# Eight-row loads for Q and K of two batches, exponents in key order, and ones matmuls at the start of a fused attention and feed-forward kernel

## The chip, the cores and the metric

The kernel runs on one core of a Trainium2 chip. A core has five engines with a queue each: TensorE (PE; its weight loads are shown as PEld), VectorE (DVE), ScalarE (ACT), GpSimd (POOL) and SyncE (SP). SP and POOL issue the DMAs, which run on the core's 16 DMA engines. The metric is device time in microseconds: 335.08 us is the median of three runs of the kernel before, which lay between 334.21 and 335.22.

## The reference

Inputs are q, k and v of eight batches, eight heads, 576 positions and 64 channels, two weight matrices (512 x 2048 and 2048 x 512) and two scalars s and b. Attention sees a window of 32 positions to each side, and its output, 4608 rows of 512, goes through a feed-forward layer:

```python
scores = scale * np.matmul(q, k.transpose(0, 1, 3, 2))
mask = np.abs(pos[:, None] - pos[None, :]) <= window          # window = 32
attn = softmax(where(mask, scores, -1e9))                     # (written out in the reference)
x = (attn @ v).transpose(0, 2, 1, 3).reshape(B * S, H * D)
h = x @ w_in
g = s * np.maximum(h, 0.0) ** 2 + b
out = g @ w_out
```

## The kernel before

**Tiling.** Heads are handled in four pairs, so that a pair's 128 channels fill TensorE's rows. Keys lie in nine tiles of 64; a tile of keys meets a window of up to 128 queries. A unit (`unit`, L534) is two key tiles (the fifth has one): for each tile, four matmuls (one for each pair) write the scores into one of two banks of PSUM, SC (L543); ACT takes the exponent into EXE or EXO (L560); then matmuls with V and a column of ones (L582) give the output and the sums (AV), DVE divides (L592, L595), and the result goes, transposed, into XT, from which the feed-forward layer reads. The keys of a pair stand in KBD, block-diagonally: head 0 in the upper 64 rows and columns, head 1 in the lower ones. Batches 0 and 1 add the band mask on TensorE before the scores (a matmul of the identity with MASKB, L549) and transpose on TensorE (L604, L607); batches 2 to 7 multiply by a mask on DVE (L564) and transpose by DMA (L612).

**Loading Q and K.** Batches 0 and 1 use `pairs_chunk` (L451): three chunks of 256, 256 and 64 positions, for all heads at once, with two neighbouring positions per partition, so a packet is 512 bytes and a chunk fills 128, 128 or 32 partitions. Staging buffer STG (nine), a cast into NAT (six), eight transposes on TensorE (L473) into a bank, and copies into QT (L479) and KBD (L490, L491). The copies into KBD write with a step of two, so that keys stand in their order; QT keeps even and odd positions apart. Batches 2 to 7 use `chunk` (L496): the same chunks, a cast on DVE (L506), a transposing DMA (L514) and copies into KBD (L521), in which even and odd keys stay apart. The exponent reads a score tile as it lies (even queries, then odd ones) and writes with a step of two. V is loaded for each head into VST (L432) and cast into VBD (L445, L446).

**The feed-forward layer.** Blocks of 128, 128, 256 and then 512 tokens. `s1` (L687) multiplies XT by w_in (L698), ACT takes the Relu (L705), DVE squares it into GT (L707). `s2` (L711) multiplies GT by w_out (L717), DVE scales and adds the constant row (L730), SP stores (L734). The constant row comes from the column sums of w_out (L740, L744). For the first three blocks the second product is made in two halves of 256 columns, as the halves of w_out come in.

**What sets the order.** Every piece of work is a task with a stream (engine), an assumed cost, reads, writes and a key. `_order` (L113) simulates the engines with the assumed costs and takes again and again the task that can start first, and among equal starts the one with the lowest key; `_rings` (L87) estimates when the DMAs land. This gives each engine its instructions in a fixed order, with semaphore waits where needed. An engine that waits holds everything behind it in its queue. Loads of batch 2 and on wait for the AV matmuls of a unit of the batch before, chosen by the tables PACE (Q and K, issued by SP) and PACEV (V, issued by POOL) (L22, L23). The first loads have rising keys from -199 on: Q and K of batch 0, V of batch 0, w_in, s and b, one half of w_out, Q, K and V of batch 1, the other half of w_out. V of batch 1 waits, besides, for the landing of one w_out load. Fills of VBD, EXO and KBD, the identity and the masks are made in the first microseconds.

Of the kernel before, what the change touches and what calls it, by code (L numbers as in the profile page):

```python
# [10 lines left out]
S = 576  # L11
# [8 lines left out]
VW = 132  # L20
XTS = 4000.0
PACE = ((0, 0, 1, 2, 3, 3), (0, 0, 1, 2, 3, 3), (0, 1, 2, 3, 3, 3))  # L22
PACEV = ((0, 0, 1, 1), (0, 0, 1, 1), (0, 1, 2, 2))  # L23
# [4 lines left out]
class _Task:  # L28
    __slots__ = ("n", "stream", "fns", "cost", "lat", "key", "deps", "users", "left",
                 "ready", "start", "fin", "dma", "sem", "seq", "val", "used", "snap", "slack")  # L30

    def __init__(self, n, stream, fns, cost, lat, key, dma, slack):
        self.slack = slack
# [9 lines left out]
class _Graph:  # L43
# [7 lines left out]
    def __init__(self, queues):  # L51
        self.queues = queues
        self.tasks = []
        self.writer, self.readers = {}, {}

    def add(self, stream, fns, cost, reads=(), writes=(), key=0.0, accum=False, dma=None, waits=(),
            lat=None, slack=0.0):
        if not isinstance(fns, list):
            fns = [fns]
        t = _Task(len(self.tasks), stream, fns, cost, self.LAT[stream] if lat is None else lat, key,  # L60
                  dma, slack)
        t.deps.update(waits)
        for r in reads:
# [14 lines left out]
        self.tasks.append(t)  # L78
        return t
# [33 lines left out]
    def _order(self):  # L113
        free = {s: 600.0 for s in self.STREAMS}
        for t in self.tasks:
            t.left = len(t.deps)
# [6 lines left out]
        while len(order) < len(self.tasks):  # L123
# [14 lines left out]
            order.append(t)  # L138
            for u in t.users:
# [97 lines left out]
def bass_sliding_window_symmetric__then__act_starrelu_kernel(  # L237
# [22 lines left out]
    with ExitStack() as es:  # L260
# [10 lines left out]
        NSTG, NNAT, NEX, NXN, NR1, NOUT, XR = 9, 6, 3, 2, 3, 3, 2048  # L271
# [5 lines left out]
        QT = [sb((128, 2, NPAIR, S // 2), BF16, "qt") for _ in range(2)]  # L277
# [92 lines left out]
        for i in range(2):  # L370
            for p0 in (0, 64):
                c0 = 64 - p0
                eng = "dve" if i == 0 else "pool"
                key = -97.0 if i == 0 else -1.0
# [8 lines left out]
        for i in range(NEX):  # L383
            for c0 in (0, 192):
                zero("dve", EXO[i][:, :, c0:c0 + 64], ("EXZ", i, c0), 220, key=-96 + i)
        add("dve", lambda e: e.tensor_copy(MASK[:, 1:4, :], MASK[:, 0:1, :].to_broadcast((128, 3, 128))),
            350, reads=[("MASKH", 1, p0) for p0 in (0, 32, 64, 96)], writes=["MASK"], key=-40)
        for pr in range(NPAIR):
            add("dve", lambda e, pr=pr: e.tensor_scalar(
                MASKB[:, pr, :].rearrange("p (i c) -> p i c", i=2), MASKH.rearrange("p (c i) -> p i c", i=2),  # L390
                1.0, 30000.0, ALU.subtract, ALU.mult),
                200, reads=[("MASKH", 0, p0) for p0 in (0, 64)], writes=[("MASKB", pr)], key=-70)
# [12 lines left out]
        def load_weights(which, i, x, key, eng):  # L405
# [6 lines left out]
            else:  # L412
# [8 lines left out]
                key=key + 20.0, slack=100.0)  # L421
# [29 lines left out]
        def pairs_chunk(b, name, t0, n, key, load_key, banks, slack=0.0):  # L451

            slot = b % 2
            si = take("stg", NSTG)
            stg = STG[si][0:n, 0:1024].rearrange("p (h i d) -> p h i d", h=H, i=2)
            add("sp", lambda e: e.dma_start(  # L456
                STG[si][0:n, 0:1024].rearrange("p (h c) -> p h c", h=H),
                src_of[name][b, :, t0:t0 + 2 * n, :].rearrange("h (p i) d -> p h (i d)", i=2)),
# [383 lines left out]
```

The softmax here doesn't subtract the row's maximum and nothing guards it: scores larger than these inputs give would overflow.

## Time and profile before

| | us |
|---|---|
| median of three runs | 335.08 |
| the profiled execution | 332.88 |
| its span | 331.1 |
| TensorE busy | 308.5 (93%) |
| VectorE busy | 206.6 (62%) |
| ScalarE busy | 166.4 (50%) |
| GpSimd busy | 87.6 (26%) |
| first matmul starts | 6.08 |
| first AV matmul starts | 19.25 |
| last matmul group starts | 326.68 |

The DMAs move 57.15 MB, 173 GB/s over the span, most of it before 240 us. A group row of the profile names the line, engine and operation, what it writes and reads, shapes, the number of instructions, then busy time and the mean of one in ns, and the idle time before them with what ended it. A wait row names who waited for whom, the total in us, how often, and the longest. In rows by stretch each engine has its busy time and, in brackets, its instructions; the granted clock of TensorE, the mean busy share of the 16 DMA engines (which passes 1 where packets overlap) and the rate follow. Rows of overlapping matmuls include the time that one waits for the one ahead of it, so a full stretch isn't yet TensorE at its peak.

### The profile page before, as it was taken

To read this page: it belongs to the slowest core of one execution; us is meant where nothing else is said; L and a number is where in the kernel's file an instruction comes from. 1 tells how busy PE (TensorE), PEld (TensorE's weight loads), DVE (VectorE), ACT (ScalarE), POOL (GpSimd) and SP (SyncE) were. 2 spreads that over 40 slices of the span, in tenths; PEclk is the share of its full clock that TensorE was granted. 3 is DMA by queue.
4 is the path that set the end of the run, shared out by engine and by line. 5 is a ranking of instruction groups with operands and counts; after the bars stand their busy time and mean duration, and the time that the engine had idled before them with its cause. 6 is when DMAs were issued, how large, how long until landed. Compare 5 with 4: busy or idle time off the path is not lost.

```text
span 331.1 us, 5839 instructions
## 1 busy us (share of the span) xinstructions
PE 308.5 (93%) x2199; PEld 179.5 (54%) x2234; DVE 206.6 (62%) x485; ACT 166.4 (50%) x270; POOL 87.6 (26%) x136
## 2 busy tenths in 40 slices
PE   1778998899999999999989999999999999999995
PEld 1567996775554555456445555555455544444442
DVE  6556564269777776898578768765874453323411
ACT  6696497229552664657175655444644433333300
POOL 8562443830910226044205500450000000000000
PEclk9999999799999999999999999999999999999999
DMA  8999999899999699979998996999811111000021
GB/s 211 224 363 357 295 195 297 219 241 167 209 202 197 193 195 206 230 170 245 173 228 163 225 212 145 247 169 213 146 56 54 56 46 62 35 32 34 32 93 68
DMA packets 107836, 57.15 MB, mean 173 GB/s; under 512 B 56608, under 2 KB 100128, under 8 KB 107808
## 3 DMA queue, kind: packets, MB, share of 16 engines
q1 hardware_dynamic: 103200, 49.69, 68.7%
q0 software_dynamic: 4608, 7.08, 11.3%
q8 instruction: 17, 0.28, 0.4%
q14 instruction: 11, 0.09, 0.1%
HBM read 36.70 MB, written 9.44 MB: 139 GB/s over the span
## 4 chain that ended last, share of the span: by engine, by line
PE 70%; DMA 13%; SPq 8%; POOL 3%; DVE 2%; ACT 2%; issue 2%; ACTq 0%
PE o L717 31%; PE w L698 29%; PE avn L582 6%; SPq L432 5%; DMA vst<-in_v_dram 5%; PE sc L543 3%; DMA stg<-in_moe_w_in_dram 3%; DMA stg<-in_moe_w_out_dram 3%; POOL vst L432 2%; SPq L456 2%; DMA out_dram<-outs 2%; ACT vbd L445 1%; SPq L416 1%; PE o L740 1%; DVE vbd L446 0%
## 5 line engine op out<-in xcount | busy, mean ns | idle before, releaser
L717 PE MATMUL o<-wout,gt 128*128 128x512 bf16 (+1 forms) x629 | 140.4, 357 | 1.9 <-DVE outs L730 1.3
L698 PE MATMUL w<-xt,win 128*128 128x512 bf16 (+2 forms) x685 | 139.8, 339 | 2.2 <-ACT r L705 1.2
L705 ACT ACTIVATE r<-w 128x512 bf16<-128x512 f32 x144 | 85.4, 598 | 95.0 <-PE w L698 80.8
L707 DVE TENSOR_TENSOR gt<-r 128x512 bf16<-128x512 bf16 x144 | 61.3, 432 | 55.1 <-ACT r L705 54.4
L717 PEld LDWEIGHTS o<-wout,gt 128*128 128x128 bf16 x640 | 61.1, 98 | 59.7 <-DVE outs L730 2.0
L698 PEld LDWEIGHTS w<-xt,win 128*128 128x128 bf16 x704 | 61.6, 98 | 52.4 <-ACT r L705 1.8
L432 POOL DMA_DIRECT2D vst<-in_v_dram x96 | 59.4, 626 | 106.8 <-PE avn L582 57.7
L730 DVE SCALAR_TENSOR_TENSOR outs<-o,sb,cvec 128x512 f32<-128x512 f32 (+1 forms) x40 | 27.7, 692 | 18.6 <-PE o L717 16.2
L560 ACT ACTIVATE exe<-sc 128x512 bf16<-128x512 f32 (+1 forms) x40 | 27.5, 687 | 15.7 <-PE sc L543 15.1
L582 PE MATMUL avn<-vbd,exo 128*128 128x130 bf16 (+1 forms) x240 | 27.9, 221 | 1.5 <-ACT xt L607 1.3
L595 DVE TENSOR_TENSOR xn<-avn,rec 128x512 bf16<-128x512 f32 (+1 forms) x38 | 26.1, 686 | 3.2 <-DMA xt<-xn 2.5
L543 PE MATMUL sc<-qt,kbd 128*128 128x128 bf16 (+1 forms) x288 | 24.8, 220 | 1.6 <-ACT exe L560 1.1
L582 PE MATMUL avn<-vbd,exe 128*128 128x130 bf16 (+1 forms) x152 | 25.3, 221 | 1.0 <-ACT vbd L445 1.0
L560 ACT ACTIVATE exo<-sc 128x512 bf16<-128x512 f32 x32 | 23.8, 743 | 4.8 <-PE sc L543 4.6
L543 PEld LDWEIGHTS sc<-qt,kbd 128*128 128x128 bf16 x288 | 20.5, 100 | 9.9 <-issue 1.0
L445 ACT CAST vbd<-vst 64x1024 bf16<-64x1024 f32 (+1 forms) x15 | 16.5, 1139 | 17.5 <-DMA vst<-in_v_dram 17.5
L582 PEld LDWEIGHTS avn<-vbd,exo 128*128 128x128 bf16 (+1 forms) x240 | 22.0, 105 | 5.5 <-ACT xt L607 1.6
L506 DVE CAST nat<-stg 128x1024 bf16<-128x1024 f32 (+1 forms) x36 | 23.7, 680 | 0.0
L521 DVE COPY kbd<-kt 64x512 bf16<-64x512 bf16 (+1 forms) x72 | 19.1, 266 | 0.8
L582 PEld LDWEIGHTS avn<-vbd,exe 128*128 128x128 bf16 (+1 forms) x152 | 16.1, 109 | 4.3 <-ACT vbd L445 1.4
L446 DVE CAST vbd<-vst 64x1024 bf16<-64x1024 f32 (+1 forms) x16 | 11.7, 745 | 7.3 <-DMA vst<-in_v_dram 7.3
L564 DVE TENSOR_TENSOR exe<-exe,mask 128x512 bf16<-128x512 bf16 (+1 forms) x30 | 11.7, 391 | 7.1 <-ACT exe L560 7.0
(63 smaller groups left out, 133.3 us busy)
## 6 DMA issues: line engine op xcount, KB each, us to landing
stg<-in_q_dram SPq DMA_DIRECT2D x16, 512.0 KB, 5.5
stg<-in_k_dram SPq DMA_DIRECT2D x16, 512.0 KB, 7.2
out_dram<-outs SPq DMA_DIRECT2D x32, 256.0 KB, 2.6
vst<-in_v_dram POOLq DMA_DIRECT2D x96, 72.0 KB, 5.5
stg<-in_moe_w_in_dram SPq DMA_DIRECT2D x8, 512.0 KB, 8.7
stg<-in_moe_w_out_dram SPq DMA_DIRECT2D x8, 512.0 KB, 8.3
vst<-in_v_dram SPq DMA_DIRECT2D x16, 144.0 KB, 4.7
stg<-in_q_dram SPq DMA_DIRECT2D x8, 128.0 KB, 6.2
```

What stands on the lines that cost most here:

```text
L432: add(stream, lambda e, dst=dst, src=src: e.dma_start(dst, src), 640.0 if stream == "sp" else 700.0, writes=[("VST", h, x) for x in (range ...
L445: add(eng, (lambda e, dst=dst, src=src: e.copy(dst, src)) if eng == "act" else (lambda e, dst=dst, src=src: e.tensor_copy(dst, src)), {"ac ...
L506: add("dve", lambda e, si=si, ni=ni: e.tensor_copy(NAT[ni][0:n, :, :].rearrange("p i (h d) -> p h i d", h=H), STG[si][0:n, 0:1024].rearran ...
L543: fns = [lambda e, j=j, pr=pr, lo=lo, hi=hi, w=w, par=par: e.matmul(SC[:, par, pr * 128:pr * 128 + w], lhsT=KBD[:, pr, j, :], rhs=QT[slot] ...
L560: add("act", lambda e, src=src, dst=dst: e.activation(dst.rearrange("p a (c i) -> p a i c", i=2), src, AF.Exp, bias=0.0, scale=0.125), 190 ...
L582: fns.append(lambda e, pr=pr, buf=buf, col=col, j=j, x=x, last=len(parts) - 1: e.matmul(av[0:nr, pr, 0:130], lhsT=buf[:, pr, col:col + nr] ...
L595: add("dve", lambda e: e.tensor_tensor(XN[xi][0:nr, :].rearrange("p (a b c) -> p a b c", a=4, b=2), av[0:nr, :, 0:128].rearrange("p a (b c ...
L698: add("pe", [lambda e, g=g, kc=kc: e.matmul(wt[:, g, :], lhsT=WIN_BF[:, kc, (f0 + g) * 128:(f0 + g + 1) * 128], rhs=XT[:, kc, t0 % XR:t0 % ...
L705: add("act", lambda e: e.activation(rt, wt, AF.Relu, bias=0.0, scale=1.0), 190 + 0.833 * 512, reads=[("W", wb)], writes=[("R1", rb)], key=key)
L707: add("dve", lambda e: e.tensor_tensor(GT[gs][:, f0:f0 + ng, g0:g0 + nt], rt, rt, ALU.mult), 130 + 0.53 * 512, reads=[("R1", rb)], writes= ...
L717: add("pe", [lambda e, fc=fc: e.matmul(O[:, ob, 0:cn], lhsT=GT[gs][:, fc, g0:g0 + 128], rhs=WOUT_BF[:, fc, c0:c0 + cn], start=(fc == 0), s ...
L730: add("dve", lambda e: e.scalar_tensor_tensor(OUTS[us][:, 0:cn], O[:, ob, 0:cn], SB128[:, 0:1], CVEC[:, c0:c0 + cn], ALU.mult, ALU.add), 2 ...
```

## The change

- Q and K of batches 0 and 1 are loaded by `load_pair` in place of `pairs_chunk`: one load for each pair of heads, all 576 positions, eight neighbouring positions per partition. A load fills 72 partitions with two packets of 2048 bytes each; there are eight in a batch instead of six. Eight transposes of 72 rows follow, one copy of 576 columns into QT, and two into KBD (DVE for the upper rows, ACT for the lower ones), which read PSUM with a step and write in order. QT of these batches has eight groups of positions instead of two, and MASKB is arranged to match.
- The exponent of every batch reads the scores in key order, with a step, and writes without one.
- Sixty matmuls of 256 columns on the ones tile, with the highest key number of all (taken last among those that can start at once), write into AVN before anything else uses it.
- A load with a key under -100 may be issued only after the one before it in the program: SP's first loads keep the order of the program. V of batch 1 has no wait of its own any more, and its units come after all its Q and K.
- PACE and PACEV let batches 2 and 3 start loading earlier; a negative entry names a unit of the batch two before.
- VBD and EXO fills and MASKB get later keys on DVE, weight casts later keys; NAT has five buffers instead of six, EXE and EXO four instead of three.

```diff
+ROWS = 8
+NWARM = 60
-PACE = ((0, 0, 1, 2, 3, 3), (0, 0, 1, 2, 3, 3), (0, 1, 2, 3, 3, 3))
-PACEV = ((0, 0, 1, 1), (0, 0, 1, 1), (0, 1, 2, 2))
+PACE = ((-1, -1, -1, 0, 1, 1), (-1, -1, 0, 1, 2, 2), (0, 0, 1, 2, 3, 3))
+PACEV = ((-1, -1, -1, -1), (0, 0, 0, 0), (0, 1, 2, 2))
...
+        after = [self.chain] if key < -100 and self.chain else []
...
+            t.left = len(t.deps) + len(t.after)
...
+            for u in t.next:
+                u.left -= 1
+                if u.left == 0:
+                    open_[u.stream].append(u)
...
-        NSTG, NNAT, NEX, NXN, NR1, NOUT, XR = 9, 6, 3, 2, 3, 3, 2048
+        NSTG, NNAT, NEX, NXN, NR1, NOUT, XR = 9, 5, 4, 2, 3, 3, 2048
...
-                key = -97.0 if i == 0 else -1.0
+                key = -57.0 if i == 0 else -1.0
...
-                zero("dve", EXO[i][:, :, c0:c0 + 64], ("EXZ", i, c0), 220, key=-96 + i)
+                zero("dve", EXO[i][:, :, c0:c0 + 64], ("EXZ", i, c0), 220, key=-50 + i)
...
-                key=key + 20.0, slack=100.0)
+                key=key + 150.0, slack=100.0)
+        def paced(b, u):
+            return land["av", b - 1, u] if u >= 0 else land["av", b - 2, NUNIT + u]
...
+        def load_pair(b, name, pr, key, load_key, banks, eng, slack):
+            n = S // ROWS
+            slot, si, ni = b % 2, take("stg", NSTG), take("nat", NNAT)
             add("sp", lambda e: e.dma_start(
+                STG[si][0:n, :].rearrange("p (h c) -> p h c", h=2),
+                src_of[name][b, 2 * pr:2 * pr + 2, :, :].rearrange("h (p i) d -> p h (i d)", i=ROWS)),
+                600.0, writes=[("STG", si)], key=load_key, dma=("l", 9, 86.0))
+            nat = NAT[ni].rearrange("p a c -> p (a c)")[0:n, :]
+            dst = nat.rearrange("p (i h d) -> p h i d", h=2, i=ROWS)
+            src = STG[si][0:n, :].rearrange("p (h i d) -> p h i d", h=2, i=ROWS)
+            add(eng, (lambda e: e.copy(dst, src)) if eng == "act" else (lambda e: e.tensor_copy(dst, src)),
+                {"act": 1040.0, "dve": 690.0, "pool": 1150.0}[eng], reads=[("STG", si)], writes=[("NAT", ni)],
+                key=key, slack=slack)
+            res, tile = banks[take("bank", len(banks))]
+            view = tile.bitcast(BF16)[:, 0:S].rearrange("p (i s) -> p i s", i=ROWS)
+            add("pe", [lambda e, i=i: e.transpose(view[:, i, :], nat[:, i * 128:i * 128 + 128], IDENT[0:n, 0:n])
+                       for i in range(ROWS)], 450.0, reads=[("NAT", ni), "IDENT"], writes=[res], key=key)
             if name == "q":
+                add("act", lambda e: e.copy(q_rows(b)[:, :, pr, :], view), 190 + 0.833 * S, reads=[res],
+                    writes=[("QT", slot, x, pr) for x in range(NTILE)], key=key)
                 return
+            for p0, ev in ((0, "dve"), (64, "act")):
+                to = KBD[p0:p0 + 64, pr, :, p0:p0 + 64].rearrange("p t (c i) -> p t c i", i=ROWS)
+                fr = view[p0:p0 + 64, :, :].rearrange("p i (t c) -> p t c i", t=NTILE)
...
-                src = src.rearrange("p a (i c) -> p a i c", i=2)
+                src = src.rearrange("p a (i c) -> p a c i", i=nrow)
...
-                    dst.rearrange("p a (c i) -> p a i c", i=2), src, AF.Exp, bias=0.0, scale=0.125),
+                    dst.rearrange("p a (c i) -> p a c i", i=nrow), src, AF.Exp, bias=0.0, scale=0.125),
...
+            for _ in range(NWARM):
+                add("pe", lambda e: e.matmul(AVN[:, 0:2, 0:128], lhsT=ONESW[:, :], rhs=ONESW[:, :].rearrange(
+                    "p (one c) -> p one c", one=1).to_broadcast((128, 2, 128)), start=True, stop=True), 110,
+                    reads=["ONESW"], writes=["AVN"], key=1e4)
-            qk(0, 0, 128)
-            qk(0, 256, 128)
+            qk(0)
             for h in range(H):
                 load_v(0, h, nxt(), "sp")
-            qk(0, 512, 32)
...
-            qk(1, 0, 128)
+            qk(1)
             for h in range(H):
-                load_v(1, h, nxt(), "sp", waits=[land["out", 2, 0]])
+                load_v(1, h, nxt(), "sp")
             cast_v(1, due(1, 0) - 4.0, (("dve", "act"), ("dve", "act")), 800.0)
-            unit(1, 0)
-            qk(1, 256, 128)
-            unit(1, 1)
-            unit(1, 2)
-            qk(1, 512, 32)
+            for m in range(NUNIT):
+                unit(1, m)
             w_out(1)
-            unit(1, 3)
-            unit(1, 4)
```

## The prediction

> **What bounds the kernel now.** I read the page's head first: the span, and how much of it TensorE fills.
>
> ```profile
> span 331.1 us, 5839 instructions
> PE 308.5 (93%) x2199; PEld 179.5 (54%) x2234; DVE 206.6 (62%) x485; ACT 166.4 (50%) x270; POOL 87.6 (26%) x136
> ...
> PE   1778998899999999999989999999999999999995
> ...
> PEclk9999999799999999999999999999999999999999
> ```
>
> TensorE is the bound, except in the first nine slices (8.3 us each) and the last. So I cut the span into stages. Columns: stretch, length, busy time (instructions) of PE, weight loads, DVE, ACT, POOL, granted clock, DMA share, GB/s.
>
> ```profile
> 0.00:6.08 6.08, 0.00 (x0) 0.00 (x0) 3.72 (x9) 4.45 (x3) 4.80 (x14) 1.00 0.69 183
> 6.08:15.60 9.52, 6.86 (x50) 5.10 (x51) 5.78 (x16) 5.77 (x10) 6.21 (x11) 1.00 1.30 239
> 15.60:19.25 3.65, 1.89 (x20) 1.09 (x18) 2.31 (x4) 3.48 (x6) 2.80 (x2) 1.00 1.09 293
> 19.25:30.00 10.75, 8.35 (x138) 7.48 (x140) 6.19 (x14) 8.46 (x16) 4.54 (x5) 1.00 1.07 374
> 30.00:50.00 20.00, 19.89 (x248) 18.27 (x248) 13.65 (x27) 14.05 (x25) 6.84 (x6) 1.00 1.14 261
> 50.00:60.00 10.00, 7.86 (x90) 6.31 (x89) 4.75 (x11) 6.45 (x13) 4.86 (x6) 1.00 1.07 300
> 60.00:63.40 3.40, 3.40 (x21) 2.58 (x19) 0.36 (x1) 0.61 (x1) 3.09 (x6) 0.50 1.04 271
> 63.40:75.00 11.60, 10.72 (x124) 9.37 (x123) 7.16 (x16) 3.71 (x6) 5.08 (x8) 1.00 1.00 207
> ...
> 170.00:312.00 142.00, 140.88 (x837) 72.12 (x852) 84.47 (x204) 65.98 (x109) 19.50 (x32) 1.00 0.56 119
> ```
>
> From 75 us on PE is full (140.88 of 142.00); only 0.9 us at 165 to 170 and the tail are lost there, and the change touches neither. What can move lies ahead of 75 us. Busy time flatters that part, because rows overlap, so I counted each recorded matmul at the full-clock pace (L740's 16 of 256 columns at 37.89 take 1.91 us, of which the last one's own 0.27: 0.109 each, and in proportion to the columns). Lag is clock time less work started: 18.7 us at 30, 19.0 at 50, 25.2 at 75. Two places make it: the start (18.7) and 50 to 75 us (6.2: 2.1 idle before 60, 1.7 in 3.4 us at clock 0.50, 0.9 idle after, the rest thin work).
>
> What PE waits for there is data: DMA's share is 1.0 or more from 6 us to 75. The rate depends on the load. Same columns, one stretch per kind: V0 (256 B packets into 64 partitions), the third q,k chunk (512 B into 32), w_in (2 KB into 128), q,k of batch 1 (512 B into 128):
>
> ```profile
> 10.00:15.00 5.00, 4.19 (x32) 3.24 (x33) 2.05 (x3) 3.35 (x6) 2.75 (x4) 1.00 1.37 205
> 15.50:17.00 1.50, 0.44 (x6) 0.37 (x6) 1.50 (x3) 1.49 (x3) 0.61 (x1) 1.00 1.20 211
> 18.00:26.00 8.00, 6.36 (x103) 5.54 (x105) 4.45 (x11) 7.15 (x14) 3.77 (x5) 1.00 1.05 387
> 34.00:41.00 7.00, 7.00 (x70) 6.23 (x69) 4.64 (x8) 3.41 (x7) 2.49 (x3) 1.00 1.14 290
> ```
>
> Last the waits, for the ends of the head:
>
> ```profile
> DVE outs L730 <- DMA out_dram<-outs: 2.3, 1, 2.3
> ...
> PE o L717 <- DVE outs L730: 1.3, 1, 1.3
> ...
> PE avn L582 <- ACT vbd L445: 1.0, 2, 0.5
> ```
>
> AV of a batch waits for V's cast, and the second product for a store stuck behind loads.
>
> **The loads, the largest term.** Q and K of one batch are 8 x 0.295 = 2.36 MB either way; now eight loads of 72 partitions with 2 KB packets, before six with 512 B. Before, batch 0 took 2.0 to 9.4 us and 15.3 to 17.0 (9.1 us), batch 1 about 34.0 to 41.8 and 1.0 later (8.8). After, no row has both properties. Lower end: 2 KB packets at 387 GB/s, 6.1 us. Upper end: 64 partitions at V0's 205 GB/s, 11.5 us. I take 211 GB/s x 9/8 = 237, or 9.9 us: the 32-partition row shows that 512 B packets fall from 290 to 211 when the tile covers part of the partitions; the large packets earn the small rise, my choice. Shift of everything behind: +0.8 us after batch 0, +1.9 after batch 1; with the ends, -3.0 and -5.7, or +2.4 and +5.1. [...]
>
> SP issues four more loads in all, 0.45 us each when not held: covered while its queue is held (3.43 us on single K issues at 29.7 and later). V0 now follows all of q and k, so it ends at 2.0 + 9.9 + 5.9 = 17.8 us, not 15.3.
>
> **Work on the loaded rows.** Casts of 1024 columns: eight instead of six, one more on POOL (1.04) and on DVE (0.69), hidden by loads 1.24 us apart. Transposes: 64 of 72 columns, 1.9 us at full clock, against 32 of 128 and 16 of 32, 2.0: nothing. Evictions: Q four times 576 columns, about 0.64 each from L479's 589 ns at 512; K the same on DVE and ACT, reading PSUM in steps, for which there is no row: 0.64 (both sides in order) to 1.4 (doubled). Only the last pair's is on the path: 0 to +0.8; I take 0.1.
>
> **Exponents.** 72 of them now read in steps and write in order. Today 743 ns with stepped writes; the Relu, 512 columns both in order, 598. Bounds: -0.145 to +0.145 us each. ACT is 57% busy at 75 to 110 us, so 1.3 us per batch either way is covered; without that cover it would be 10 us over the kernel. In batch 0, nine stand in a row: -1.3 to +1.3, I take -0.6.
>
> **The start.** Last K lands near 2.0 + 9.9 + 1.1 = 13.0; cast, transposes and eviction 1.9 more; SC at 15, its nine exponents until about 21; V0's casts (DVE 0.75, ACT 1.04) end near 19.7, so AV(0,0) goes from 19.25 to about 19.8. But then the other units follow each 0.9 us (0.20 + 0.69 on DVE), because no third chunk lies in between: today they start at 19.25, 20.13, 23.5, 25.1 and 28.8. w_in comes 0.8 later; its first quarter is cast near 23. PE would be full from 23.7 with 9.1 us of work done (1.9 transposes, 4.0 SC, 3.2 AV): lag 14.6 against 18.7. ACT's and DVE's queues will not fit so neatly: I take 15.7, a gain of 3.0. Ends: 0 and -5.
>
> **The ones matmuls.** Sixty of 256 columns: 0.109 us each at full clock, 0.20 at half (L740 at 59.7: 16 in 3.3), so 6.5 to 12 us from about 1.2 us. All are PE's lowest priority in the plan, but PE keeps order, so the first transposes (6.08 today) may wait until 7 to 9; the last pair's, due at 13.7, is what counts: 0 to +1, taken as 0. They warm PE: today L549 with 512 columns takes 0.63 us at 12 to 15 us and 0.39 from 17. [...] Worth 0.3 us of the 3.0.
>
> **Fills, buffers, order, pacing.** The V fills (3 x 1.02 us on DVE) go behind the K casts; two more EXO fills, 0.17 each: covered by 17 us until V0. Five NAT and four E buffers: the E one lets SC of batch 1 run ahead of V1. V1's dropped wait was on a load that had landed by 36; V1 was issued at 40.6: nothing. SP's forced order is nearly today's. Batch 2 loads (issued at 55 to 73 today) may start sooner, as may batch 3's; this puts them ahead of stores on SP: 0 to +2 at 50 to 60, and up to -1 at 75 to 80.
>
> **50 to 75 us.** Work ready before V1: batch 0 10.4, first product of three blocks 14.0, half the second 8.8, batch 1 transposes and SC 5.0: 38.2. With lag 15.7 PE is dry at 53.9; AV(1,0) can start at 54.3 + 1.9 = 56.2: 2.3 us idle. Stores 1.3, half clock 0.9 (even odds of 1.7), thin work 0.6: 5.1, against 6.2 today, a gain of 1.1.
>
> **Sum.** -3.0 - 1.1 = -4.1. The profiled execution, 332.88 us (span 331.1 and 1.8 around it), becomes 328.8; the median is 2.2 above it, so 335.08 - 4.1 = 331.0.
>
> **Rivals.** *Loads at full rate* (6.1 us): the wait for V1 goes (-2.3) and the start gains 2 more: 326.7. For it: only packet size. *No change*: the head is bound by bytes, w_out's second half lands 2 us later, and PE loses at V1 what it won at the start (3.0 + 1.1): 335.1. For it: DMA's share of 1.0 to 75 us. *Slower*: the written order counts a pair load as 9 x 86 = 0.77 us; at 1.24 the second batch's transposes stand 3.7 us too early in PE's queue, and PE waits there with second-product work behind. It decides from a stall of 4.1 us, that is a load batch of 10.3 us; at 11.5 the stall is 5.3 and the start 1.6 worse: 331.0 + 6.9 = 337.9. Against it: other work may have been ordered ahead. *The warm-up does nothing*, the clock falling back before SC: +0.3, inside the forecast.
>
> **Numbers.** Forecast (328 to 334) 0.44, full rate 0.18, no change 0.14, slower 0.24. Faster 0.62, same 0.14 (within 0.3%, 1.0 us, about what a measurement can tell), slower 0.24. The range, 325 to 338, leaves about one in ten on each side.
>
> **What would show it.** Rate in 3 to 11 us near 237 GB/s (387 or 205 for the rivals); AV(0,0) near 20 and five units by 25; full clock before 10; a wait of 2 us before AV(1,0); PE idle on transposes near 45 us would be the slower rival. I am wrong if the full stage from 75 us changes length.

## The result, and the profile after

| | before | after |
|---|---|---|
| median of four runs, us | 334.64 | 346.74 |
| lowest and highest | 333.97, 335.22 | 346.02, 348.80 |
| profiled execution (its span) | 332.88 (331.1) | 347.10 (345.4) |

The ratio is 1.037, with a 95% interval of 1.032 to 1.042: the change makes the kernel 12 us slower. The forecast was 4 us faster, and the range ended at 338. Here and below a ratio leaves out executions more than 1.5% above the fastest of their kernel; the medians hold all.

The head of the page, for the kernel after:

```profile
span 345.4 us, 6028 instructions
...
PE 318.9 (92%) x2291; PEld 185.6 (54%) x2326; DVE 204.3 (59%) x485; ACT 159.6 (46%) x262; POOL 89.7 (26%) x138
...
PE   8687768968999989999979999999999999999996
...
PEclk9769999999999999999999999999999999999999
```

Of the busy time of PE, 10.7 us are the group of the ones matmuls. The digits say where to look: the slices from 26 to 86 us hold 6, 7 and 8, but for one 9, where all were 8 or 9 before. By stretch (the columns as before: busy time of PE, weight loads, DVE, ACT, POOL, then clock, DMA share, GB/s):

```profile
6.08:15.60 9.52, 7.03 (x88) 5.67 (x87) 4.38 (x12) 3.82 (x6) 4.33 (x8) 0.84 0.92 196
15.60:22.38 6.78, 5.48 (x42) 3.35 (x40) 4.51 (x14) 4.03 (x7) 4.50 (x7) 0.50 0.96 200
22.38:30.00 7.62, 6.10 (x92) 5.54 (x94) 4.18 (x9) 5.42 (x10) 3.12 (x4) 0.97 1.02 369
30.00:50.00 20.00, 15.02 (x187) 12.08 (x184) 9.50 (x20) 9.67 (x16) 5.56 (x6) 1.00 0.95 259
50.00:60.00 10.00, 8.60 (x108) 7.26 (x107) 5.89 (x12) 4.71 (x8) 2.08 (x2) 0.83 0.92 190
60.00:70.00 10.00, 9.14 (x100) 7.69 (x101) 3.92 (x9) 7.99 (x13) 8.35 (x14) 1.00 1.10 296
70.00:80.00 10.00, 5.51 (x68) 4.30 (x65) 4.29 (x9) 2.90 (x6) 5.91 (x7) 1.00 1.13 251
80.00:170.00 90.00, 87.78 (x629) 50.99 (x641) 68.86 (x176) 46.59 (x80) 30.70 (x48) 1.00 1.02 196
170.00:312.00 142.00, 139.41 (x839) 71.71 (x855) 85.96 (x207) 64.13 (x107) 20.36 (x32) 1.00 0.62 128
```

PE was full from 30 to 50 us (19.89 of 20.00) and is now busy for 15.02. Before, it had no wait in that stretch; now it has these:

```profile
PE o L726 <- DVE cvec L753: 1.0, 1, 1.0
PE sc L489 <- ACT r L714: 0.7, 1, 0.7
PE sc L489 <- DVE nat L484: 0.7, 1, 0.7
PE avn L612 <- DVE xn L603: 0.6, 1, 0.6
PE avn L590 <- ACT xt L615: 0.5, 1, 0.5
PE o L726 <- DVE wout L432: 0.5, 1, 0.5
PE o L726 <- POOL wout L432: 0.4, 1, 0.4
PE o L612 <- DVE xn L603: 0.2, 1, 0.2
PE o L749 <- POOL wout L432: 0.2, 1, 0.2
```

They are 4.9 us in nine pieces, none over 1.0, ended by casts of w_out and of batch 1's K and by other work of DVE and ACT. The DMAs moved 239 and 293 GB/s before the first AV; now 196 and 200.

The prediction's lag (clock time less work started) makes a finer ruler. From here on it counts, besides the recorded matmuls, those whose record is missing but whose weight load is there, and leaves the ones matmuls out; its late values are good to some 3 us, the differences between two kernels to about 1:

| lag, us, at | 20 | 30 | 40 | 50 | 60 | 70 | 80 | 120 | 140 | 180 | 325 |
|---|---|---|---|---|---|---|---|---|---|---|---|
| before | 15.0 | 18.7 | 18.7 | 19.0 | 22.3 | 24.0 | 25.7 | 26.3 | 26.4 | 27.4 | 27.9 |
| after | 17.1 | 20.9 | 24.0 | 27.7 | 31.1 | 32.4 | 37.5 | 38.3 | 40.1 | 42.0 | 42.1 |
| lost | 2.1 | 2.2 | 5.3 | 8.7 | 8.8 | 8.4 | 11.8 | 12.0 | 13.7 | 14.6 | 14.2 |

So nothing was won at the start; 8.8 us were lost by 60, 3 more between 70 and 80, and 2.4 behind that. The spans differ by 14.3. One trace has its limits: single executions of the kernel before lay between 330.1 and 338.2 over the sets below, so a difference of under 3 us between two traces proves little.

When data arrives is read from the casts that wait for it. DVE's casts of K (batch 0, then batch 1), in the timeline of the kernel after (start, length, instruction, idle time before it and what ended it):

```profile
5.90 0.69 DVE L484 CAST nat<-stg 72x1024 bf16<-72x1024 f32 x1 [0.56 <-DMA stg<-in_k_dram]
...
15.36 0.69 DVE L484 CAST nat<-stg 72x1024 bf16<-72x1024 f32 x1 [1.37 <-DMA stg<-in_k_dram]
...
45.34 0.69 DVE L484 CAST nat<-stg 72x1024 bf16<-72x1024 f32 x1 [3.86 <-DMA stg<-in_k_dram]
...
54.53 0.69 DVE L484 CAST nat<-stg 72x1024 bf16<-72x1024 f32 x1 [1.71 <-DMA stg<-in_k_dram]
```

From the first to the last K six loads land, 1.58 us each in batch 0 and 1.53 in batch 1, or 187 and 193 GB/s for 0.295 MB, with some of V among them. V of batch 0 is cast from 20.9 on (before: 15.7), V of batch 1 from 58.4 (52.4), and the second column sum of w_out starts at 76.1 (59.7).

### The profile page after: what moved, and what is told of

Its sections match the earlier page's. It is cut to its first block, busy times and chain, and to the rows that moved or that the text cites. A ratio compares the mean times of both kernels' runs of the same rounds, so it can differ in the third digit from the quotient of the medians.

```text
span 345.4 us, 6028 instructions
## 1 busy us (share of the span) xinstructions
PE 318.9 (92%) x2291; PEld 185.6 (54%) x2326; DVE 204.3 (59%) x485; ACT 159.6 (46%) x262; POOL 89.7 (26%) x138
## 4 chain that ended last, share of the span: by engine, by line
PE 69%; DMA 13%; SPq 10%; POOL 3%; DVE 2%; issue 1%; ACT 1%; ACTq 0%
PE o L726 31%; PE w L707 29%; SPq L449 9%; PE avn L590 5%; DMA vst<-in_v_dram 5%; DMA stg<-in_moe_w_out_dram 5%; PE sc L551 3%; POOL vst L449 3%; DMA xt<-xn 2%; DMA stg<-in_moe_w_in_dram 2%; SPq L477 1%; DVE vbd L463 1%; DVE outs L739 0%; SPq L508 0%; ACT win L432 0%
## 5 line engine op out<-in xcount | busy, mean ns | idle before, releaser
L726 PE MATMUL o<-wout,gt 128*128 128x512 bf16 (+1 forms) x627 | 143.2, 358 | 3.9 <-DVE outs L739 1.3
L707 PE MATMUL w<-xt,win 128*128 128x512 bf16 (+2 forms) x686 | 142.7, 341 | 2.6 <-ACT r L714 1.6
L716 DVE TENSOR_TENSOR gt<-r 128x512 bf16<-128x512 bf16 x144 | 59.5, 419 | 57.3 <-ACT r L714 56.7
L707 PEld LDWEIGHTS w<-xt,win 128*128 128x128 bf16 x704 | 62.3, 98 | 54.7 <-ACT r L714 2.8
L449 POOL DMA_DIRECT2D vst<-in_v_dram x96 | 61.2, 645 | 111.2 <-PE avn L590 110.1
L739 DVE SCALAR_TENSOR_TENSOR outs<-o,sb,cvec 128x512 f32<-128x512 f32 (+1 forms) x40 | 27.6, 692 | 16.7 <-PE o L726 16.6
L568 ACT ACTIVATE exe<-sc 128x512 bf16<-128x512 f32 (+1 forms) x40 | 22.2, 555 | 13.1 <-PE sc L551 13.0
L462 ACT CAST vbd<-vst 64x1024 bf16<-64x1024 f32 (+1 forms) x15 | 16.7, 1140 | 15.2 <-DMA vst<-in_v_dram 15.0
L463 DVE CAST vbd<-vst 64x1024 bf16<-64x1024 f32 (+1 forms) x16 | 12.7, 811 | 14.5 <-DMA vst<-in_v_dram 14.4
L568 ACT ACTIVATE exo<-sc 128x512 bf16<-128x512 f32 x32 | 19.1, 597 | 2.8 <-PE sc L551 2.7
L529 DVE COPY kbd<-kt 64x512 bf16<-64x512 bf16 (+1 forms) x72 | 18.4, 255 | 0.8
L600 DVE RECIPROCAL rec<-avn 128x8 f32<-128x8 f32 (+1 forms) x38 | 7.7, 203 | 15.8 <-PE avn L590 15.5
```

Of the source, the lines that this page charges most:

```text
L449: add(stream, lambda e, dst=dst, src=src: e.dma_start(dst, src), 640.0 if stream == "sp" else 700.0, writes=[("VST", h, x) for x in (range ...
L529: add("dve", lambda e, i=i, p0=p0: e.tensor_copy(KBD[p0:p0 + 64, :, j0:j0 + nj, p0 + 32 * i:p0 + 32 * i + 32], KT[p0:p0 + 64, i, :, t0 // ...
L568: add("act", lambda e, src=src, dst=dst: e.activation(dst.rearrange("p a (c i) -> p a c i", i=nrow), src, AF.Exp, bias=0.0, scale=0.125), ...
L707: add("pe", [lambda e, g=g, kc=kc: e.matmul(wt[:, g, :], lhsT=WIN_BF[:, kc, (f0 + g) * 128:(f0 + g + 1) * 128], rhs=XT[:, kc, t0 % XR:t0 % ...
L716: add("dve", lambda e: e.tensor_tensor(GT[gs][:, f0:f0 + ng, g0:g0 + nt], rt, rt, ALU.mult), 130 + 0.53 * 512, reads=[("R1", rb)], writes= ...
L726: add("pe", [lambda e, fc=fc: e.matmul(O[:, ob, 0:cn], lhsT=GT[gs][:, fc, g0:g0 + 128], rhs=WOUT_BF[:, fc, c0:c0 + cn], start=(fc == 0), s ...
```

## Experiments

The theories: the *rate* of a load that fills 72 partitions; that every unit now *waits for all eight* loads; the *order and pacing* of what comes behind; and single *waits* that the trace names at 70 to 80 us.

**The loads by themselves.** A kernel of nothing but loads, eight of a kind, kind after kind.

```diff
+    [two_rows(i, 128) for i in range(8)],
+    [two_rows(i, 32) for i in range(8)],
+    [eight_rows(i, 0, 72) for i in range(8)],
+    [eight_rows(i, 32, 72) for i in range(8)],
+    [eight_rows(i, 56, 72) for i in range(8)],
+    [eight_rows(i, 0, 64) for i in range(8)],
+    [eight_rows(i, 64 * (i % 2), 64) for i in range(8)],
+    [weights(i) for i in range(8)],
+    [eight_rows(i, 56 * (i % 2), 72) for i in range(8)],
```

> This kernel only loads and computes nothing: nine stages on an otherwise empty chip, each of eight loads on SP's queue, each stage waiting for the one before. In order: two-row chunks into 128 partitions (4.19 MB), the same into 32 (1.05 MB), eight-row pairs into partitions 0 to 71 (2.36 MB, as in the changed kernel), into 32 to 103, into 56 to 127, eight-row pairs of 64 partitions from 0 (2.10 MB), the same alternating between 0 and 64, w_in into 128 (4.19 MB), and eight-row pairs alternating between 0 to 71 and 56 to 127. Theory 1, the place of the tile limits the rate (half of the partitions give half of the rate): 0 to 71, 56 to 127 and 64 from 0 all near 200 to 240 GB/s, 32 to 103 and both alternating stages clearly faster, 280 or more, w_in near 385. Theory 2, a load of 72 rows is shared out badly among the DMA engines: all four stages of 72 near 200 to 290 whatever the place, both stages of 64 near 385. Theory 3, the loads are only slow because other work disturbs them: all eight-row stages near 385.

Stretches inside the stages of one execution (POOL idle; then clock, DMA share, GB/s), in the order of the diff: 128 partitions and 32 partitions with 512-byte packets; eight rows into 72 partitions from 0, from 32, from 56; 64 partitions from 0; 64 in turn from 0 and 64; w_in, 128 partitions with 2 KB packets; 72 in turn from 0 and 56.

```profile
3.00:16.00 13.00, 0.00 (x0) 1.00 1.19 296
20.00:23.00 3.00, 0.00 (x0) 1.00 1.06 203
27.00:36.50 9.50, 0.00 (x0) 1.00 0.80 217
40.00:48.50 8.50, 0.00 (x0) 1.00 0.77 253
53.00:61.50 8.50, 0.00 (x0) 1.00 0.80 217
65.00:74.00 9.00, 0.00 (x0) 1.00 1.06 224
78.00:85.50 7.50, 0.00 (x0) 1.00 1.06 239
89.00:99.00 10.00, 0.00 (x0) 1.00 1.02 356
104.00:112.50 8.50, 0.00 (x0) 1.00 0.80 216
```

The pair loads are slow by themselves, so the third theory falls: with packets four times larger they lose a quarter of the rate (217 against 296), and with packets of the same 2 KB a tile of 128 partitions runs at 356. Two things come together. 64 partitions from 0 are slow with all engines busy: 224 at a share of 1.06. And tiles of 72 partitions hold the share at 0.77 to 0.80, from 0, from 32, from 56 and in turn. The share times 16 is the mean number of packets in flight, and with the rate it gives the time of one 2 KB packet (estimates from these rows): 16 packets of 94 ns for 128 partitions, 17 of 155 ns for 64 from 0, 12 of 100 ns for 72 from 32, 13 of 121 ns for 72 from 0. So 72 from 32 loses by fewer packets in flight, 64 from 0 by slower packets, and the tile of the change by both. Neither of the other theories gives all of this: the first wanted 280 or more for 72 from 32 and for both stages in turn (253, 239, 216), the second 385 for 64 partitions. The pair load stands with the tiles of 32 and 64 partitions. A tile that avoids both losses with eight rows to a partition was not tried.

**The change with chunk loads in place of pair loads**: forced order, ones matmuls, new pacing, keys and buffers are kept, and the third chunk is loaded ahead of V. The diff is against the changed kernel.

```diff
-ROWS = 8
+ROWS = 2
...
-        def load_pair(b, name, pr, key, load_key, banks, eng, slack):
+        def pairs_chunk(b, name, t0, n, key, load_key, banks, slack=0.0):
...
```

> The changed kernel with Q and K of batches 0 and 1 loaded in the two-row chunks of the kernel before (128, 128 and 32 partitions); the forced order, ones matmuls, exponents, pacing and buffers stay as changed. If the slow loads are the cause, the 12 us come back: 331 to 335 us, a little under the kernel before if the other parts help. If the cause is the forced order, the pacing or the ones matmuls: 342 to 347.

342.87 us, ratio 1.027 (1.017 to 1.036), in the range of the other parts and not of the loads. The lag at 60 us is 22.9, almost that of before: the head is mended, and yet two thirds of the loss are still there, behind 60 us.

**The pair loads alone**: the kernel before with these loads and the key-order exponents; batch 1's Q and K stand ahead of its units. The diff is against the changed kernel; keys, buffers and the wait of V of batch 1 are as before, too.

```diff
-NWARM = 60
-PACE = ((-1, -1, -1, 0, 1, 1), (-1, -1, 0, 1, 2, 2), (0, 0, 1, 2, 3, 3))
-PACEV = ((-1, -1, -1, -1), (0, 0, 0, 0), (0, 1, 2, 2))
+NWARM = 0
+PACE = ((0, 0, 1, 2, 3, 3), (0, 0, 1, 2, 3, 3), (0, 1, 2, 3, 3, 3))
+PACEV = ((0, 0, 1, 1), (0, 0, 1, 1), (0, 1, 2, 2))
...
-        after = [self.chain] if key < -100 and self.chain else []
+        after = []
...
```

> The kernel before with the eight-row pair loads of batches 0 and 1 (and what they need: QT's layout, batch 1's Q and K all ahead of its units) and key-order exponents; old pacing, no forced order, no ones matmuls, six NAT and three E buffers, old keys, V of batch 1 with its wait. Theory L (the rate of a 72-partition load, 211 instead of 290 GB/s, is the whole loss, by data that comes later and lags that are never made up): 342 to 348 us, the lag at 50 us 25 or more and growing little after 80. Theory D (load shape costs 4 to 5 us, and the rest is pacing and order): 337 to 341, the lag at 140 us under 34. Under 336 the load shape costs nothing without the rest.

350.66 us, ratio 1.048 (1.040 to 1.055): +16 us, more than the whole change and more than either theory gave. The lag at 50 is 28.4, as theory L had it, but it grows from 33.5 at 80 to 42.2 at 120 and 44.4 at 180, which L excludes. PE from 80 to 100 us:

```profile
80.00:100.00 20.00, 16.24 (x125) 9.74 (x126) 13.52 (x36) 10.88 (x18) 3.15 (x6) 1.00 0.75 143
```

The DMAs move 143 GB/s here at a share of 0.75; before, 197 at 1.09. The loads of batch 3 are late: POOL issues its V from 96.8 us on (before: 82.2), SP its first Q from 96.6 (84.0). V waits, by the old pacing, for a unit of batch 2; on SP it is transposing DMAs ahead of Q that stand, 11 us between 80 and 100, for work of DVE.

**The pacing alone**, in the kernel before.

```diff
-PACE = ((0, 0, 1, 2, 3, 3), (0, 0, 1, 2, 3, 3), (0, 1, 2, 3, 3, 3))
-PACEV = ((0, 0, 1, 1), (0, 0, 1, 1), (0, 1, 2, 2))
+PACE = ((-1, -1, -1, 0, 1, 1), (-1, -1, 0, 1, 2, 2), (0, 0, 1, 2, 3, 3))
+PACEV = ((-1, -1, -1, -1), (0, 0, 0, 0), (0, 1, 2, 2))
...
```

> The kernel before with the new pacing tables alone. Theory P (loads of batch 2 and 3 that start sooner crowd out w_out's second half and the first products, whatever the rest is): 338 to 344 us, the V loads of batch 2 issued by POOL before 62 us, the second column sum later than 62 us, the lag at 80 us 28 or more. Theory D: the old order has room for it, 334 to 337, lag at 80 us within 1.5 of 25.7. Earlier loads as a gain: under 333.5.

342.81 us, ratio 1.023 (1.018 to 1.029): +8 us, in theory P's range, and the lag at 80 is 29.5; but P's way is wrong. POOL issues V at 56 to 69 us, as before, and the second column sum is at 59.6 (59.7). The loss begins here:

```profile
77.66 1.42 DVE L450 CAST vbd<-vst 64x1024 bf16<-64x1024 f32 x2 [6.92 <-DMA vst<-in_v_dram]
78.39 2.20 ACT L449 CAST vbd<-vst 64x1024 bf16<-64x1024 f32 x2 [6.03 <-DMA vst<-in_v_dram]
```

DVE and ACT stand 6 to 7 us at the casts of V of batch 2. Q and K of batch 2 are now issued 3 to 11 us sooner and share the DMA engines with V (that this delays V is argued, not shown). Behind the DVE cast is a division, and PE waits 4.7 us for that.

**The change with the old pacing**, of both tables, and of V alone.

```diff
-PACEV = ((-1, -1, -1, -1), (0, 0, 0, 0), (0, 1, 2, 2))
+PACEV = ((0, 0, 1, 1), (0, 0, 1, 1), (0, 1, 2, 2))
```

> The changed kernel with the pacing tables of Q, K and V of the kernel before; all else changed. Theory A, a second cause beside the load shape is that batch 2's sixteen V issues (10.1 us of GpSimd) stand ahead of three w_out casts, and that batch 3's loads stand ahead of transposing DMAs: 337 to 342. Theory B, the load shape and what follows from it is all: 345 to 348.

> The changed kernel with only the V pacing of the kernel before. Theory A, with GpSimd's queue as its main part: 340 to 344, and the column sums of the second half of w_out start well before 76 us. If the early Q and K loads are the harmful ones: 345 to 348, while the kernel with both old tables is faster.

Both are slower than the change: 356.22 us (1.065; 1.059 to 1.071) and 357.21 (1.070; 1.065 to 1.074). The reason for trying them was POOL's queue in the kernel after:

```profile
61.66 1.04 POOL L432 CAST wout<-stg 128x1024 bf16<-128x1024 f32 x1 [7.05 <-DMA stg<-in_moe_w_out_dram]
62.64 10.14 POOL L449 DMA_DIRECT2D vst<-in_v_dram  x16
72.77 3.26 POOL L432 CAST wout<-stg 128x1024 bf16<-128x1024 f32 x3
```

Sixteen issues of V, 0.63 us each, stand ahead of three casts, and PE waits 1.3 us at 76 us for the last. With the old order of V the lag at 80 us is indeed 5 us smaller (32.4 instead of 37.5). But it is 43.3 at 120: V of batch 2 is issued at 71.5 to 81.8, and everything of batches 2 and 3 is late. The new pacing is worth 9 us in this kernel (1.037 against 1.065) and costs 8 in the kernel before. It belongs to the pair loads; it is a partial repair of their loss, not its cause.

**Chunk loads and the old pacing.** The change without its two large parts; the edit is the chunk loads of above with the old tables.

> The changed kernel with both other suspects undone: two-row chunk loads for batches 0 and 1, and the old pacing of batches 2 and 3; forced order, ones matmuls, key-order exponents, buffers and keys as in the change. Theory D (load shape and pacing together make the loss, and neither alone can be put right because the plan was laid out for both): 333 to 337 us, PE's lag at 80 us 25 to 27 and at 140 us under 30. Theory E (the forced order, the keys and the dropped wait on V of batch 1 cost some 8 us by themselves): 341 to 346, with the lag at 80 us near 29, as with chunk loads and the new pacing. Above 346 us the old pacing hurts here as it did with the pair loads (+9), and the new pacing was needed for the new order.

340.28 us, ratio 1.014 (1.008 to 1.021): between the theories, nearer to E. Forced order, keys, buffers, ones matmuls and the order of batch 1 together still cost 5 us; the lag at 80 is 28.7, against 25.7. The parts roughly add up (the order of batch 1 stands in both): pair loads 16 and the rest 5 make 21, where the change with the old pacing measured 22; the new pacing takes 9 of that back, and 12 are left. So the pair loads are the main loss. With chunk loads the new pacing costs 4 (1.027 against 1.014).

**The ones matmuls**, taken out of the change and put alone into the kernel before.

```diff
-NWARM = 60
+NWARM = 0
```

> The changed kernel without the 60 ones matmuls. If they fill time in which TensorE waits for loads anyway: 346 to 348, within 1 us of the changed kernel. If they hold up the transposes: 343 to 345. If the clock that they raise is worth something: 347.5 to 350, with the first attention units later.

> The kernel before with the sixty ones matmuls alone. If the early clock is worth something: 333.0 to 334.3 us, the granted clock full by 7 us instead of 15.9, the first AV before 19.25. If the clock falls back before the scores come, as it did at 12.85 us in the changed kernel: no difference within 0.3%. If the first transposes queue behind them: up to +1.

Without them the change takes 352.01 us (its four executions spread from 346.4 to 356.3; 1.041; 1.027 to 1.054), so they aren't the loss. Alone they make the kernel before slower by 0.5% (0.15 to 0.9%). The first transposes are held up: they start at 7.95 us instead of 6.08, right behind the ones, and the first scores at 11.59 instead of 10.70. That is made up: the first AV comes at 19.35 (19.25), and the lag is the same as before at 65 to 75 us and parts from it only behind that, by less than two traces can tell. In that kernel the clock is full from 4.6 to 18.3 us, over the scores, and still nothing is won; it is half from there to 21.7 (mean over 15 to 35 us 0.91). In the kernel after it is full from 5.7 us and half again from 12.5 to 22.8 (the rows above: 0.84, then 0.50). In the 4 us ahead of that fall PE was busy for 2.1 and stood for 1.9, in pieces of 0.93 at most.

**The exponents alone**, in the kernel before.

```diff
-                src = src.rearrange("p a (i c) -> p a i c", i=2)
+                src = src.rearrange("p a (i c) -> p a c i", i=2)
...
-                    dst.rearrange("p a (c i) -> p a i c", i=2), src, AF.Exp, bias=0.0, scale=0.125),
+                    dst.rearrange("p a (c i) -> p a c i", i=2), src, AF.Exp, bias=0.0, scale=0.125),
```

> The kernel before with nothing changed but the exponents, which read in key order with a step and write in order. The instruction of 512 columns should take about 600 ns instead of 743. If ScalarE is covered, as I forecast: 334 to 335.5, no difference; if its shorter turns reach TensorE in the head: 332 to 334.

No difference: 334.73 us against 334.79, ratio 1.002 (0.997 to 1.007), though each gets faster, from a mean of 743 ns to this:

```profile
L560 ACT ACTIVATE exo<-sc 128x512 bf16<-128x512 f32 x32 | 19.2, 600 | 3.6 <-PE sc L543 3.5
```

**The assumed cost of a pair load.** The rival *Slower* said that the written order reckons with loads that are too quick.

```diff
-                600.0, writes=[("STG", si)], key=load_key, dma=("l", 9, 86.0))
+                600.0, writes=[("STG", si)], key=load_key, dma=("l", 9, 160.0))
```

> The changed kernel, but the planner is told 160 ns instead of 86 for each of a pair load's nine rows of packets, 1.44 us instead of 0.77 for a load, about what the trace shows; only the order of each engine's instructions can change. If part of the loss is TensorE standing at work that was ordered too early: 340 to 344. If the loss is only the later arrival of the data: 345.5 to 348.

348.84 us, ratio 1.043 (1.034 to 1.052). The lag at 60 is 2.7 smaller than in the change, at 80 it is 37.4, as there (37.5). With the right cost in the plan the loss stays.

**The named waits behind 70 us.** Casts of w_out's second half away from POOL, and casts of V of batches 2 to 7 later in the order: in the change, in the kernel before with the new pacing, and in the change with the dearer loads.

```diff
-                    load_weights("out", i, x, nxt(), ("pool" if x else ("dve", "pool")[i % 2]))
+                    load_weights("out", i, x, nxt(), (("act", "dve")[i % 2] if x else ("dve", "pool")[i % 2]))
```

```diff
-                cast_v(b, due(b, 0) - 4.0, (("dve", "act"), ("dve", "act")), 3000.0)
+                cast_v(b, due(b, 0) - 4.0, (("dve", "act"), ("dve", "act")), 8000.0)
```

> The changed kernel with the new pacing, but the four casts of the second half of w_out on ScalarE and VectorE in turn instead of GpSimd, so that no V issue stands ahead of them. Theory A: 341 to 344, as with the old V pacing, the second column sums near 66 to 70 us instead of 76. Theory B: 345 to 348.

> The changed kernel with one number of the plan changed: the casts of V of batches 2 to 7 are ordered as if their data landed 8 us later than the plan thinks, not 3. Theory H (DVE and ACT stand at these casts, 3.7 us at 78, and hold up what feeds TensorE): no wait of DVE on V there, the lag at 80 us falls from 37.5 to 34 to 35.5, the time to 342 to 344.5. Theory N (TensorE has nothing else to do there anyway, because the data is late): the wait goes and the time stays within 1.5 us of 346.7. Higher if batch 2 itself is now late.

> The kernel before with the new pacing alone (342.8 us), and the casts of V of batches 2 to 7 ordered 5 us later in the plan. There DVE stood 6.9 us at such a cast, until 77.7, and TensorE waited 4.7 us for what was behind it. Theory H: the wait goes and with it 4 to 7 us: 336 to 339, lag at 80 us 26 to 27. Theory N: above 341.

> The changed kernel with both corrections of the plan's times: pair loads at 1.44 us each instead of 0.77 (alone 348.8 us, but a lag 2.7 us smaller at 60) and the casts of V of batches 2 to 7 ordered 5 us later. Theory H: the gain of the head stays, 340 to 343. Theory N: 346 to 349.

351.83 us (1.051; 1.047 to 1.055), 350.00 (1.043; 1.035 to 1.051), 344.07 (1.026; 1.020 to 1.032) and 349.06 (1.039; 1.032 to 1.046), none faster than the kernel that it was made from. With w_out cast elsewhere the second column sum starts at 72.1 instead of 76.1 and PE's wait for POOL is gone, but PE stands 2.2 us at 80 for a division on DVE. With the pacing alone, DVE's wait of 6.9 us falls to 0.4, the lag at 80 is 27.1 (29.5 with the wait), and at 120 it is 38.8 (36.0). PE's longest waits at 75 to 125 us are now these:

```profile
PE sc L547 <- DVE kbd L525: 3.2, 2, 1.8
PE avn L586 <- DVE exo L568: 2.8, 2, 2.4
```

Theory H, that these casts carry the loss, fell in all three: what PE waits for next is late too.

**Three quarters of the bytes** of the pair loads, the rest of the change as it is. The kernel leaves out two of a partition's eight rows, which stay zero.

```diff
-                STG[si][0:n, :].rearrange("p (h c) -> p h c", h=2),
-                src_of[name][b, 2 * pr:2 * pr + 2, :, :].rearrange("h (p i) d -> p h (i d)", i=ROWS)),
+                STG[si][0:n, :].rearrange("p (h c) -> p h c", h=2)[:, :, 0:384],
+                src_of[name][b, 2 * pr:2 * pr + 2, :, :].rearrange("h (p i) d -> p h (i d)", i=ROWS)[:, :, 0:384]),
...
```

> The changed kernel with three quarters of the bytes of the pair loads: packets of 1536 bytes, six of a partition's eight rows (the other two are zeros, so scores are wrong for a quarter of the positions); number of loads, partitions, issues, transposes, copies and the written order of work as in the change, the casts a quarter shorter. Theory R (the rate into 72 partitions makes the loss of the first 50 us): loads of batch 0 land near 12 us instead of 15, the lag at 50 us falls from 27.7 to 22 to 24, and the time to 338 to 342. Theory G (every unit waits for all eight loads, and the order around them): the lag at 50 us stays above 26 and the time above 344.

345.34 us, ratio 1.029 (1.020 to 1.038). The first AV starts 2.6 us sooner, so bytes do set the start. But the lag at 50 is 27.5, where theory R wanted 22 to 24: between 33.6 and 41.8 us PE now stands, 5.2 us in three pieces, at second products whose quarters of w_out come no sooner (first cast at 36.1 us, in the change at 36.3). At 60 it is 28.4, 2.7 less than in the change; the stop before 80 takes that back.

**A lower rate, in the kernel before**: each 128-partition load of Q and K issued as two of 64 partitions, or four of 32. SP issues 8 or 24 loads more for that.

```diff
+            parts = 2 if n == 128 else 1
+            m, deps, more = n // parts, (), []
+            for x in range(parts):
+                add("sp", lambda e, x=x: e.dma_start(
+                    STG[si][x * m:x * m + m, 0:1024].rearrange("p (h c) -> p h c", h=H),
+                    src_of[name][b, :, t0 + 2 * m * x:t0 + 2 * m * x + 2 * m, :].rearrange("h (p i) d -> p h (i d)", i=2)),
...
```

> The kernel before with each 128-partition load of Q or K of batches 0 and 1 issued as two loads of 64 partitions (lower half, then upper half); bytes, packets of 512 bytes, casts, transposes, copies, units and pacing as before. By themselves such loads in turn ran at 231 GB/s, against 290 for the whole. Theory R (rate alone): 2.1 MB in each batch take 9.1 us instead of 7.2, so some 1.9 us in each batch: the rate over 2 to 60 us falls from 288 to 275 to 282 GB/s, the lag at 60 us rises by 2 to 4, and the time by 2 to 5 us, to 337 to 340. Theory G (what matters is that a unit waits for all eight loads): within 1 us of before.

> The same with four loads of 32 partitions each, which ran at 210 GB/s by themselves: about the rate of the pair loads (211). Theory R: 10.0 us instead of 7.2 in each batch, the rate over 2 to 60 us down to 255 to 275 GB/s, the lag at 60 us up by 4 to 8, the time 339 to 346. Theory G: within 2 us of before (SP issues 24 loads more, 0.45 us each). If halves cost something and quarters no more than halves, it is the issuing and not the rate.

342.61 us (1.027; 1.023 to 1.031) and 344.59 (1.029; 1.024 to 1.035): 9 and 10 us, though no unit waits for more than before and nothing but the loads was cut. From 2 to 60 us, the kernel with halves:

```profile
2.00:60.00 58.00, 42.82 (x483) 35.83 (x487) 33.73 (x72) 37.55 (x61) 23.52 (x33) 0.97 1.07 254
```

The halves fell below the rate expected (275 to 282), the quarters stayed in it (267), above the halves. The two times can't be told apart; by the recorded expectation that speaks for the issuing on SP and against the rate. But quarters add three times as many issues as halves and lose no more by 60 us, so the issuing doesn't order them either, and these runs don't separate the two. My scale from the isolated rates was wrong, and why quarters bring more than halves was not shown. The sizes of the lag at 60 (3.0 and 1.9 over before) were near the forecast for the halves and under it for the quarters; most of the time went later, as in all the others.

**All together.** Mean rate from 2 to 60 us, the lag at 60 over that of before, and what the span lost besides:

| kernel | GB/s | by 60 us | behind 60 us |
|---|---|---|---|
| before | 288 | 0 | 0 |
| pacing alone | 285 | 0.0 | 10.0 |
| chunks, old pacing | 282 | 1.4 | 6.3 |
| chunks, new pacing | 280 | 0.6 | 7.7 |
| ones matmuls alone | 279 | 0.8 | 3.4 |
| quarters | 267 | 1.9 | 11.0 |
| halves | 254 | 3.0 | 6.8 |
| after | 240 | 8.8 | 5.5 |
| pair loads alone | 234 | 9.6 | 7.0 |
| three quarters of the bytes | 232 | 6.1 | 6.5 |

From 280 GB/s down, the less arrives the larger the lag at 60, but for the last row, which has 1.18 MB less to fetch. A late kernel also issues batch 2's loads later (from 60.1 us after, 55.0 before), which lowers the mean; but up to 50 us, ahead of any such load, it is 285 before, 262 with halves and 250 after. By 60 us the kernel before has moved 288 x 58 = 16.7 MB, the one after 13.9: the head of this kernel runs as fast as bytes arrive. Two things stay open. The halves and quarters pay 1.5 to 1.6 us for each MB that is missing at 60, the kernels with pair loads 2.9 to 3.2; so at the price of the former half of the 8.8 us, 4.3, is the rate, and the rest may be that all units wait for all eight loads, or a price that rises with the shortage. And behind 60 us nearly every new order loses 3 to 12 us, each at other waits; no single cause was found.

No version beat the kernel before; the one with key-order exponents equals it.

## Why the prediction was wrong

In lag, 18.6 us lie between forecast and trace: 5.2 at the start, 6.8 from 30 to 50 us, 2.2 from 50 to 75 and 4.4 behind. The step that failed first is the rate of the pair loads; the largest is the stretch from 30 to 50 us that was taken as full.

- *What bounds the kernel* was right: data, up to 75 us.
- *The loads* (9.9 us at 237 GB/s): the step that failed first. The casts show about 1.55 us for a load, 12.4 us for eight, above the upper end of 11.5; alone such loads ran at 217. The last K of batch 0 was cast at 15.4 us, where 13.0 was forecast for its landing. The term "the large packets earn the small rise" was a choice without a row, and the rows next to it (205, 211) had it right: alone, 64 partitions from 0 gave 224 and 72 from 0 gave 217. They don't give the 253 of 72 partitions from 32 on, where fewer packets were in flight (12, against 17 with 64 from 0).
- *The start* (lag 15.7 at 30): 20.9. AV(0,0) came at 22.4, not 19.8, and the units did not follow each 0.9 us: 22.4, 23.0, 27.5, 29.1, 32.2. I named the risk ("queues will not fit so neatly") and gave it 1.1 us.
- *30 to 50 us*: the sum has PE full from 23.7 to 53.9 and the lag unchanged. It grew from 20.9 to 27.7, by the nine waits shown above and the thin work between them. The prediction moved what lies behind the loads by 0.8 and 1.9 us and didn't ask which of PE's work would stand at it.
- *50 to 75 us* (5.1 us lost): 7.3, from a lag that began at 27.7 instead of 19. The wait of 2 us before AV(1,0) didn't come: it came at 65.9, not 56.2, behind other work, and PE's waits from 50 to 66 us were 1.3 at transposes and 0.8 at scores.
- *Order and pacing* (0 to +2 at 50 to 60, up to -1 at 75 to 80): a mis-sized term. The order, keys, buffers and ones together cost 5 us with chunk loads. The pacing alone costs 8 us, at 76 to 110 us, but with the pair loads it is worth 9. I had counted SP's queue only, not POOL's, where 10.1 us of V issues stand ahead of the casts of w_out, nor DVE's and ACT's, where casts of V hold up what feeds PE.
- *From 75 us on* "the change touches neither": wrong, and the sentence that would show it was on record. The lag grew by 7.1 us from 75 to the end (before: 2.7).
- *The ones matmuls*: worth nothing, as the rival "the warm-up does nothing" had it; the clock fell back at 12.5 us, before the scores (18.0). The 0.3 us that the forecast gave them no run shows. The clock isn't the whole reason, since alone they kept it full over the scores and won nothing either. Alone they cost 0.5%, not 0.
- *Exponents* and *work on the loaded rows*: right. Key-order exponents take 597 ns, at the lower end, and move nothing; evictions of Q take 0.64 us, those of K 0.63 (ACT) and 0.73 to 0.74 (DVE), near the lower end of 0.64 to 1.4.
- *Slower* (0.24) had the sign, and PE does stand at transposes of batch 1, 2.7 us in three pieces from 45 to 56. But its cause, the plan's cost of a pair load, wasn't the one: corrected, it moved 2.7 us at 60 and nothing at the end.

## What to carry to other kernels

In this kernel, whose head is bound by bytes, a load's partitions, how many and which, mattered more than the size of its packets (2 KB into 72 partitions 217 or 253 GB/s, 512 B into 128 partitions 296): measure the rate of the very tile before building on larger packets. The pacing table fitted one arrival of data: it cost 8 us with the old loads and was worth 9 with the pair loads, and removing a wait that a trace named showed only the next one (four kernels, none faster). When a load is issued sooner, look at every in-order queue that holds work for its data, the issuing engine's (10.1 us of V issues ahead of POOL's casts of w_out) and the casting engines' (6.9 us of DVE at a cast of V), not only at the queue that it moves in.

## What was not expected of the hardware

- Eight rows into 72 partitions: 217 GB/s from partition 0 or 56, 253 from 32, all at a DMA share of 0.77 to 0.80, that is 12 or 13 packets in flight where tiles of 64 and 128 had 16 to 19.
- Loads of 64 partitions in turn from 0 and from 64 gained little over those from 0 alone: 239 against 224.
- The exponent of 512 columns loses 146 ns to a stepped bf16 write (743 to 597), and nothing to a stepped read of PSUM (597, where the Relu with both in order takes 598).
- The clock fell to half at 12.5 us in the kernel after, with PE busy for 2.1 of the 4 us ahead and no gap on it over 0.93.
- Cutting a load in two lowered the rate over 2 to 60 us from 288 to 254; cutting it in four, only to 267.
